# Gated linear attention and a mixer on one core: batch 2's scaled q and k turned by transposing transfers, with a new hand-written order

## The chip, the cores and the metric

One Trainium2 chip, one of its cores. A core has a matrix engine (PE, with its weight loads PEld), three engines for elementwise work (DVE, ACT, POOL), a queue engine (SP) that here only issues transfers, and 16 DMA engines that move data between HBM and the on-chip memory (SBUF). PE writes to eight banks of accumulator memory (PSUM), from which DVE and ACT copy results out. The metric is the device time of one execution in microseconds (us), lower is better; it is told as the median of several runs.

## What is computed

Four batches of 768 tokens. Per batch an attention with eight heads of 48 and a decaying state, then a mixer: two products over the tokens, a residual, two products over the channels, a residual.

```python
# attention: batch 4, heads 8, tokens 768, head size 48
f = 1.0 / (1.0 + np.exp(-f_logit))
for t in range(S):
    state = f[:, :, t, :, None] * state + einsum('bhd,bhe->bhde', k[:, :, t], v[:, :, t])
    y[:, :, t] = einsum('bhd,bhde->bhe', q[:, :, t], state)
# mixer on x = y as [4, 768, 384]; w_tok 768x256 and 256x768, w_ch 384x1536 and 1536x384
h = np.maximum(x.transpose(0, 2, 1) @ w_tok1, 0.0) @ w_tok2
u = x + h.transpose(0, 2, 1)
out = u + np.maximum(u @ w_ch1, 0.0) @ w_ch2
```

Inputs and output are float32; the products run in bf16 with float32 accumulation.

## The kernel before

Each batch's 768 tokens are six chunks of 128. For a chunk the kernel takes the logarithms of the gates (`gates`: Exp and Ln on ACT, and `Llo`, the low half of a split into two bf16 parts, by a subtraction on DVE or POOL) and sums them over the chunk's tokens by a product with a triangular matrix (the "sums", L516 to L531). From the sums ACT makes two factors, `G` and `Gi` (L541, L543). DVE multiplies q by the one and k by the other into the tile `qk` (L562). Scores within the chunk need q and k with the head dimension on the partitions, so `qk`, 128 tokens by 1024, must be turned into `qkT`. There are two ways in the code:

- on PE (L579): eight 128x128 products with the identity into one PSUM bank, which DVE then copies to `qkT` (L592);
- by a transposing transfer (L569), issued on SP, from `qk` straight to `qkT`. A placeholder on PE that issues nothing (`hold`) reserves the PSUM bank that the scores will use.

`TURNED` says from which batch on the second way is taken: 3, so batch 3 alone. Then come the scores (L476), their masking on DVE (`AmT`, L616), the products of k and v for the state (`parts`, L492), the state's update on DVE (L628 to L633) and its copies (`state_bd`), and the output `y` (L651, L658). The state needs the last row of the chunk's factor spread over the partitions in another way; from batch 1 on ACT writes it to `ends` (L550) and a small transfer on SP carries it over to `glast` (L556, called `across`). Batches 1 to 3 handle chunks in pairs.

The mixer of a batch (`mixer`) has the token products (L693, L709), the residual (L725), a copy to bf16 (`u_bf`), a turn of it to `uT` (on PE and DVE for batches 0 and 1, by two transfers, L739, for batches 2 and 3), the first channel product with its ReLU (`ch1`, L768, L439 and L441), and the second (`ch2`, L787) with residual (L793) and output (L797, 192 KB per tile of 128 tokens, on SP).

The inputs are loaded by POOL in a fixed sequence (L360, L367); batch 0's gates by SP and ACT. There are four sets of `qk`/`qkT`, taken by the chunk's number modulo 4: chunks 0 to 3 take sets 0 to 3, chunks 4 and 5 sets 0 and 1, and the next batch begins with set 0 again.

Work is not issued where it is written down. Every piece of work is an operation with its possible engines, what it needs and makes, and a cost (`kind`), and gets a running number. The table `ORDER`, written out by hand, lists all 1116 operations: code // 4 is the operation's number, code % 4 picks one of its engines. `best` goes through `ORDER`, gives each operation a start by the costs, gives out the PSUM banks, and fills gaps on PE before 25.5 us with dummy products (L834). The operations are then issued in the order of these starts. Each engine works strictly in its order and waits at an operation until what it needs is there. So on one engine the order is that of `ORDER`; the costs act only on the choice of banks and on the number of dummies. Cost entries that matter here: `("fix", own, end)` occupies its engine for `own` ns and is done after `end`; a fourth number made a transfer occupy a common wire.

Of the kernel before, what the change touches and what calls it, by code (L numbers as in the profile page):

```python
# [20 lines left out]
TURNED = 3  # L21
ORDER = (
# [60 lines left out]
)  # L83
KEPT = 3
SPLIT = 5
SLOTS = (5110, 5800, 7500, 8450, 9600, 10400, 11400, 13000, 14400, 14800, 16700,
         18000, 19100, 19500, 20000, 20700, 21400, 23400, 24300, 25900)
HELD = (2600, 3600, 4100, 4750, 5500, 6500)


class Op:
# [18 lines left out]
class Plan:  # L110
# [65 lines left out]
    def best(self, idle, cold, until):  # L176
# [10 lines left out]
        for code in ORDER:  # L187
# [47 lines left out]
            elif op.kind[0] == "fix" and len(op.kind) > 3:  # L235
                wire = max(wire, t + 1000) + op.kind[3]
                if op.kind[3] > 1000:
                    op.end = max(op.end, wire + 1200)
# [629 lines left out]
```

## Time and profile before

| | |
|---|---|
| time, median of 3 runs | 172.79 us (171.46 to 176.41) |
| span of the profiled execution | 170.2 us |
| granted PE clock in it | 1.000 |
| instructions | 4181 |
| HBM read, written | 25.17 MB, 4.72 MB |
| busy POOL | 99.3 us (58%) |
| issue of one transposing transfer, `qkT`, on SP | 1.31 us, median of 6 |
| issue to landing of an output tile, `across`, `uT` | 3.1, 4.0, 2.8 us, medians |

The profile shows one execution. The span runs from the first to the last instruction; the measured times also hold what lies around it. "Busy" is the time in which an engine had work, and PE's pieces overlap in its pipeline, so the latency of one product is longer than the distance between two. A row of a group reads: line, engine, operation, what is written and read, how often; then busy us and mean ns of one; then how long the engine had been idle before, and on what. For a transfer the landing is counted from its issue.

### The profile page before, as it was taken

The numbers are of one execution on the slowest core, as the hardware profiler recorded it, in microseconds if no ns is written. First come the engines' busy times: TensorE is split into PE (matmuls) and PEld (weight loads), VectorE is DVE, ScalarE is ACT, GpSimd is POOL, SyncE is SP. The second block draws the span as 40 slices with busy tenths as digits, with TensorE's granted clock in tenths as the row PEclk, the third lists the DMA queues.
The fourth block names the chain that finished last, engine by engine and source line by source line (L and its number), as shares of the span: only waits on it lengthen the run. The fifth ranks groups of instructions, "written<-read, shape, count | busy, mean of one in ns | idle before, by whom it ended". The sixth has DMA issues, their size and how long they took to land.

```text
span 170.2 us, 4181 instructions
## 1 busy us (share of the span) xinstructions
PE 162.9 (96%) x1606; PEld 102.8 (60%) x1606; DVE 128.0 (75%) x287; ACT 108.2 (64%) x256; POOL 99.3 (58%) x134
## 2 busy tenths in 40 slices
PE   6899999999999999999999999999999999999992
PEld 2356565665766576665776756665666666566661
DVE  5679995966898998899999868768884723675431
ACT  4759993598879889999999978385545320510100
POOL 7999569896499969999978869603111200000000
PEclk9999999999999999999999999999999999999999
DMA  6999999999999997999998999996920060220253
GB/s 103 141 174 149 156 192 181 212 149 201 192 167 136 161 165 75 116 155 133 182 157 49 134 251 107 144 165 115 228 100 4 0 139 0 92 96 0 78 202 139
DMA packets 102547, 22.71 MB, mean 133 GB/s; under 512 B 95264, under 2 KB 101664, under 8 KB 102528
## 3 DMA queue, kind: packets, MB, share of 16 engines
q0 software_dynamic: 79440, 13.77, 101.8%
q1 hardware_dynamic: 22560, 8.59, 22.5%
q8 instruction: 12, 0.20, 0.5%
q10 hardware_dynamic: 528, 0.10, 0.3%
q14 instruction: 7, 0.06, 0.1%
HBM read 25.17 MB, written 4.72 MB: 176 GB/s over the span
## 4 chain that ended last, share of the span: by engine, by line
PE 64%; DMA 12%; DVE 7%; ACT 6%; POOL 6%; issue 2%; SPq 1%; DVEq 0%; POOLq 0%
PE ps L768 22%; PE ps L787 22%; DMA v_sb<-in_v_dram 5%; PE ps L709 4%; POOL qk_sb L360 4%; PE ps L693 4%; DMA glast<-ends 4%; DMA out_dram<-x_nat 3%; DVE AmT L616 2%; PE ps L476 2%; PE ps L579 2%; PE ps L658 2%; POOL v_sb L360 1%; PE ps L530 1%; PE ps L651 1%
## 5 line engine op out<-in xcount | busy, mean ns | idle before, releaser
L787 PE MATMUL ps<-w_ch,zT 128*128 128x384 bf16 (+2 forms) x300 | 51.6, 320 | 0.0
L768 PE MATMUL ps<-uT,w_ch 128*128 128x384 bf16 x288 | 50.6, 326 | 0.0
L439 ACT ACTIVATE zT<-ps 128x384 bf16<-128x384 f32 x56 | 25.3, 494 | 25.3 <-PE ps L768 25.2
L768 PEld LDWEIGHTS <-w_ch 128*128 128x128 bf16 x288 | 27.7, 98 | 17.7
L787 PEld LDWEIGHTS <-zT 128*128 128x128 bf16 x300 | 27.9, 98 | 16.9
L616 DVE TENSOR_TENSOR AmT<-ps,tri_bf 128x512 bf16<-128x512 f32 x46 | 30.5, 686 | 2.5 <-PE ps L476 2.3
L441 DVE TENSOR_SCALAR zT<-ps 128x384 bf16<-128x384 f32 x40 | 21.1, 554 | 8.8 <-PE ps L768 8.8
L360 POOL DMA_DIRECT2D v_sb<-in_v_dram x24 | 22.2, 925 | 4.1 <-DMA w_ch<-in_moe_w_ch_dram 4.1
L360 POOL DMA_DIRECT2D qk_sb<-in_k_dram x24 | 22.4, 932 | 0.8 <-POOLq L852 0.8
L360 POOL DMA_DIRECT2D qk_sb<-in_q_dram x24 | 22.3, 930 | 0.0
L793 DVE TENSOR_TENSOR x_nat<-x_nat,ps 128x384 f32<-128x384 f32 (+2 forms) x25 | 13.3, 535 | 10.6 <-PE ps L787 10.2
L360 POOL DMA_DIRECT2D f_sb<-in_f_logit_dram x18 | 16.5, 943 | 0.2
L562 DVE TENSOR_TENSOR qk<-qk_sb,GG 128x768 bf16<-128x768 bf16 (+1 forms) x30 | 14.2, 475 | 2.1 <-ACT GG L543 1.0
L450 ACT ACTIVATE f_sb<-f_sb 128x384 f32<-128x384 f32 x24 | 12.5, 524 | 4.6 <-DMA f_sb<-in_f_logit_dram 4.4
L434 POOL CAST state_bd<-state 48x192 bf16<-48x192 f32 x13 | 4.5, 347 | 16.2 <-DVE state L633 14.6
L725 DVE TENSOR_TENSOR x_nat<-x_nat,ps 128x384 f32<-128x384 f32 x21 | 10.5, 550 | 3.4 <-PE ps L709 3.1
L834 PE MATMUL ps<-steady 128*128 128x512 bf16 x30 | 11.3, 483 | 1.7 <-DVE steady L375 1.7
L543 ACT ACTIVATE GG<-ps 128x384 bf16<-128x384 f32 x24 | 11.6, 489 | 2.0 <-PE ps L531 1.9
L541 ACT ACTIVATE GG<-ps 128x384 bf16<-128x384 f32 x24 | 11.7, 488 | 1.4 <-PE ps L531 1.2
L579 PE MATMUL ps<-ident,qk 128*128 128x128 bf16 x144 | 11.6, 224 | 0.0
L579 PEld LDWEIGHTS <-qk 128*128 128x128 bf16 x144 | 9.2, 100 | 2.7 <-DVE qk L562 0.7
L550 ACT ACTIVATE ends<-ps 32x384 f32<-32x384 f32 x15 | 7.0, 481 | 4.9 <-PE ps L531 4.7
(81 smaller groups left out, 234.1 us busy)
## 6 DMA issues: line engine op xcount, KB each, us to landing
out_dram<-x_nat SPq DMA_DIRECT2D x23, 192.0 KB, 3.1
f_sb<-in_f_logit_dram POOLq DMA_DIRECT2D x18, 192.0 KB, 5.4
qk_sb<-in_k_dram POOLq DMA_DIRECT2D x24, 96.0 KB, 5.1
qk_sb<-in_q_dram POOLq DMA_DIRECT2D x24, 96.0 KB, 4.9
v_sb<-in_v_dram POOLq DMA_DIRECT2D x24, 96.0 KB, 5.5
w_ch<-in_moe_w_ch_dram POOLq DMA_DIRECT2D x2, 576.0 KB, 7.5
w_ch<-in_moe_w_ch_dram POOLq DMA_DIRECT2D x1, 1152.0 KB, 10.6
f_sb<-in_f_logit_dram SPq DMA_DIRECT2D x5, 192.0 KB, 4.7
```

What stands on the lines that cost most here:

```text
L360: lambda eng=eng, into=into, of=of: eng.dma_start(out=into, in_=of),
L439: nc.scalar.activation(out_, in_, AF.Relu, bias=0.0, scale=1.0)
L441: nc.vector.tensor_scalar(out_, in_, 0.0, None, ALU.max)
L450: add(ACT, r, lambda: nc.scalar.activation(fb, fb, AF.Exp, bias=0.0, scale=-1.0), make=[key], kind=el, need=([("fb", c)] if c < 1 else []) ...
L541: add(ACT, r, lambda: nc.scalar.activation(G[i], sview(), AF.Exp, bias=0.0, scale=-1.0), make=[("G", i)], bank=p_s, kind=el)
L543: add(ACT, r, lambda: nc.scalar.activation(Gi[i], sview(), AF.Exp, bias=0.0, scale=1.0), make=[("Gi", i)], bank=p_s, kind=el)
L562: add(DVE, r, lambda n=n: nc.vector.tensor_tensor(qk[i4][:, n, :, 0:D], qk_sb[nb][:, n, :, c, :], GG[i][:, n], ALU.mult), need=[(x, nb, c) ...
L579: nc.tensor.transpose(to[:, o + hp, :], blk(src)[:, hp, :], ident)
L616: add(DVE, r, lambda half=half, made=made: nc.vector.tensor_tensor(half, made(), tb4, ALU.mult), need=["tri_bf"], make=[("AmT", i, p)], ba ...
L768: nc.tensor.matmul(banks[pm.at][:, 0:384], lhsT=w[:, kt, c0:c0 + 128], rhs=uT[:, th, :, kt, :], start=(kt == 0), stop=(kt == 2))
L787: nc.tensor.matmul(banks[pm.at][:, 0:n1 - n0], lhsT=zT[:, kt, tt * 128:(tt + 1) * 128], rhs=w_ch2[:, kt, n0:n1], start=(kt == 0), stop=(kt ...
L793: add(DVE, rank("ch2", tt), lambda un=un, pm=pm, n=n1 - n0: nc.vector.tensor_tensor(un, un, banks[pm.at][:, 0:n], ALU.add), make=[("x_nat" ...
```

## The change

- `TURNED` is 2 instead of 3: batch 2's `qk` is turned by transposing transfers too. Its six chunks lose eight products on PE and one DVE copy each, and get one transfer on SP and one placeholder on PE.
- The placeholder no longer needs the transfer, so it may reserve its bank before the transfer has landed.
- The sets of `qk`/`qkT` are numbered through the batches, `(b * NCH + c) % NQ` with `NQ = 4`, so that a set comes around every four chunks also where one batch follows another.
- In the planner transfers of a `fix` kind no longer occupy a common wire; they have fixed landing times, with new numbers for `across`, the transposes and the outputs, and a transpose of the mixer's or the attention's kind waits in the plan for the last but one before it.
- `ORDER` is new as a whole. The numbers of the operations mean what they meant, except that in each chunk of batch 2 the two operations of the turn are now a transfer and a placeholder, and that in batch 3 these two have changed places.

```diff
-TURNED = 3
+TURNED = 2
+NQ = 4
 ORDER = (
...
 )
...
+        turned: list = []
...
+            if op.kind[0] == "fix" and len(op.kind) > 3 and len(turned) > 1:
+                t = max(t, turned[-2])
...
-            elif op.kind[0] == "fix" and len(op.kind) > 3:
-                wire = max(wire, t + 1000) + op.kind[3]
-                if op.kind[3] > 1000:
-                    op.end = max(op.end, wire + 1200)
+            elif len(op.kind) > 3 and op.kind[0] == "fix":
+                turned.append(op.end)
...
-        need = [("qkT", c % 4, p) for c in cs for p in range(2)]
+        need = [("qkT", (b * NCH + c) % NQ, p) for c in cs for p in range(2)]
...
-        i, i4, nb, g4 = c % 2, c % 4, b % NB, (b * NCH + c) % 4
+        i, i4, nb, g4 = c % 2, (b * NCH + c) % NQ, b % NB, (b * NCH + c) % 4
...
-                kind=("fix", 600, (5200, 5200, 3400)[b - 1], 300))
+                kind=("fix", 500, (6000, 5200, 4500)[b - 1]))
...
         if b >= TURNED:
+            add(SP, r, lambda: nc.sync.dma_start_transpose(out=qkT[i4], in_=qk[i4].rearrange("t n h d -> t (n h d)")),
+                need=[("qh", i4), ("kh", i4)], make=[("qkT", i4, 0), ("qkT", i4, 1)], kind=("fix", 1350, 6500, 1))
             hold = Bank()
-            add(SP, r, lambda: nc.sync.dma_start_transpose(out=qkT[i4], in_=qk[i4].rearrange("t n h d -> t (n h d)")),
-                need=[("qh", i4), ("kh", i4)], make=[("qkT", i4, 0), ("qkT", i4, 1)], kind=("fix", 1900, 6000, 1700))
-            add(PE, r, lambda: None, need=[("qkT", i4, 0)], make=[("hold", b, c)], bank=hold, kind=("mm", 1))
+            add(PE, r, lambda: None, make=[("hold", b, c)], bank=hold, kind=("mm", 1))
             return [hold, Bank()]
...
-                make=[("uT", 3 * th + j, d) for j in range(3) for d in range(3)], kind=("fix", 1900, 6000 if b > 2 else 8000, 1900))
+                make=[("uT", 3 * th + j, d) for j in range(3) for d in range(3)], kind=("fix", 1400, 4000 if b > 2 else 7200, 1))
...
-                    need=[("x_nat", xn, tt, n0) if end else ("x_nat", xn, tt)], kind=("fix", 350, 2000, 580))
+                    need=[("x_nat", xn, tt, n0) if end else ("x_nat", xn, tt)], kind=("fix", 420, 4500 if b < 3 else 2000))
```

What the new `ORDER` holds that the prediction speaks of, read from its codes:

- Eight ReLUs of batch 1 are given to DVE instead of ACT, two of batch 0 too; in batches 2 and 3 five go from DVE to ACT. In batch 0, two copies to `qkT`, one of `y`, one of `u_bf` and one of `uT` go from DVE to ACT, and one of the state's copies from ACT to DVE. In batches 2 and 3 four of the copies to `x_bf` go from DVE to ACT.
- On PE the order of the stages is as before, with other interleaving. Between the sums of batch 2's chunk 1 and the scores of chunks 0 and 1 stand one token product (two products), 18 turns of `u_bf`, the sums of chunks 2 and 3 and 14 `ch1` groups of three products.
- On SP, the transfers around batch 2 run: transpose of chunk 0, its `across`, output of batch 0's tile 5, transpose of chunk 1, output of tile 4, `across` of chunk 2, transposes of chunks 2 and 3, `across` of chunks 1 and 3, transposes of chunks 5 and 4, `across` of chunk 4, output of batch 0's tile 3, transposes of batch 3's chunks 0 and 1.
- On POOL the loads keep their sequence. The two `Llo` of batch 2 that POOL makes are those of chunks 2 and 3, before those of chunks 1 and 0.
- The last group on PE is the third part of batch 3's tile 0, 384 columns, with its residual and output behind it; before, it was tile 5's last 96 columns.

More of the change, by code (lines that the diff above doesn't have):

```diff
@@ L300 @@
     G, Gi = [t[:, 0] for t in GG], [t[:, 1] for t in GG]
-    qk = [st([128, 2, H, 64], BF16, f"qk{i}") for i in range(4)]
+    qk = [st([128, 2, H, 64], BF16, f"qk{i}") for i in range(NQ)]
     qh, kh = [t[:, 0] for t in qk], [t[:, 1] for t in qk]
-    qkT = [st([128, 8, 128], BF16, f"qkT{i}") for i in range(4)]
+    qkT = [st([128, 8, 128], BF16, f"qkT{i}") for i in range(NQ)]
     AmT = [st([128, 8, 128], BF16, f"AmT{i}") for i in range(2)]
@@ L411 @@
         once(DVE, lambda i=i: nc.vector.memset(state_bd[i], 0.0), [("sbd", i)], 220)
-    for i in range(4):
-        once(DVE, lambda i=i: nc.vector.memset(ends[i][96:128, :, D:64], 1.0), [("ends", i)], 200)
+    for i in range(NQ):
+        if i < 4:
+            once(DVE, lambda i=i: nc.vector.memset(ends[i][96:128, :, D:64], 1.0), [("ends", i)], 200)
         for n, tl in (("qh", qh[i]), ("kh", kh[i])):
@@ L480, in attention @@
             own = 212 if k else 330
-            chain = add(PE, due(b, cs[0]), lambda c=c, k=k: scores(c % 4, heads[k]), need=need, bank=heads[k][1],
+            chain = add(PE, due(b, cs[0]), lambda c=c, k=k: scores((b * NCH + c) % NQ, heads[k]), need=need, bank=heads[k][1],
                         kind=("mm", own if live and b else own + 107, own), tail_of=chain)
@@ L491, in parts @@
                     hp, par = h // 2, h % 2
-                    nc.tensor.matmul(dg(k)[par * 64:par * 64 + 64, hp, :], lhsT=kh[c % 4][:, h, :],
+                    nc.tensor.matmul(dg(k)[par * 64:par * 64 + 64, hp, :], lhsT=kh[(b * NCH + c) % NQ][:, h, :],
                                      rhs=v_sb[nb][:, h, c, :], start=b > 0 or (c == 0 and hp == 0), stop=True,
@@ L496, in attention @@
         if live and b == 0:
-            add(PE, due(b, cs[0]), parts, need=[("kh", cs[0] % 4), ("v", nb, cs[0])], make=["sums"], bank=p_d,
+            add(PE, due(b, cs[0]), parts, need=[("kh", cs[0] % NQ), ("v", nb, cs[0])], make=["sums"], bank=p_d,
                 kind=("mm", 345, 238))
         elif live:
-            chain = add(PE, due(b, cs[0]), parts, need=[("kh", c % 4) for c in live] + [("v", nb, c) for c in live],
+            chain = add(PE, due(b, cs[0]), parts, need=[("kh", (b * NCH + c) % NQ) for c in live] + [("v", nb, c) for c in live],
                         bank=p_d, kind=("mm", 230 + 115 * len(live), 123 + 115 * len(live)), tail_of=chain)
@@ L597, in rest @@
     def rest(b, c, r, p_a, p_d, dg):
-        i, i4, nb, g4 = c % 2, c % 4, b % NB, (b * NCH + c) % 4
+        i, i4, nb, g4 = c % 2, (b * NCH + c) % NQ, b % NB, (b * NCH + c) % 4
         last = c == NCH - 1
```

120 rows, old and new, of the table ORDER are left out of this document.

## The prediction

> **What bounds the kernel now.** I read the page first, then the busy time by stretch.
>
> ```profile
> span 170.2 us, 4181 instructions
> PE 162.9 (96%) x1606; PEld 102.8 (60%) x1606; DVE 128.0 (75%) x287; ACT 108.2 (64%) x256; POOL 99.3 (58%) x134
> ```
>
> ```profile
> 0.00:20.00 20.00, 17.52 (x183) 9.10 (x183) 15.41 (x52) 13.67 (x34) 17.32 (x28) 1.00 1.90 142
> 20.00:25.00 5.00, 4.82 (x87) 3.40 (x84) 4.74 (x13) 4.80 (x12) 3.02 (x5) 1.00 1.61 187
> 25.00:32.00 7.00, 6.51 (x67) 4.14 (x66) 5.09 (x12) 4.20 (x11) 6.87 (x9) 1.00 1.14 209
> ...
> 45.00:60.00 15.00, 14.61 (x181) 9.73 (x180) 13.68 (x30) 12.43 (x30) 14.84 (x18) 1.00 2.13 154
> 60.00:75.00 15.00, 14.87 (x170) 10.03 (x169) 14.01 (x32) 14.19 (x36) 13.54 (x17) 1.00 1.52 127
> 75.00:90.00 15.00, 15.00 (x192) 10.35 (x192) 14.60 (x32) 14.71 (x37) 13.37 (x17) 1.00 1.86 150
> ...
> 120.00:135.00 15.00, 14.76 (x150) 9.47 (x149) 10.91 (x24) 6.85 (x15) 2.65 (x8) 1.00 0.37 88
> ...
> 150.00:166.90 16.90, 16.83 (x116) 10.50 (x113) 8.49 (x18) 1.36 (x3) 0.00 (x0) 1.00 0.29 108
> 166.90:170.20 3.30, 0.00 (x0) 0.00 (x0) 0.22 (x1) 0.00 (x0) 0.00 (x0) 1.00 0.32 110
> ```
>
> PE is busy for 96% of the span. Columns of the second fence: stretch, length, then busy PE, weight loads, DVE, ACT, POOL, the granted clock and the DMA share. There are three parts. Up to about 32 us PE is not the limit: it is filled up with L834 dummies (11.3 us, row below) while loads, DVE and ACT deliver batch 0. From 32 to 166.9 PE never rests: its idle time in the rows from 25 us on is 0.49 + 0.39 + 0.13 + 0.24 + 0.07 = 1.3 us, at full clock. The last 3.3 us are the tail: last residual, last output. So a microsecond of PE work removed after 32 us is worth a microsecond, as long as what replaces it arrives in time. In 60 to 90 us there is little room beside PE: DVE is busy 28.6 of 30 us, ACT 28.9.
>
> **What is removed.** Batch 2's scaled q and k are turned on PE (L579, eight 128x128 per chunk) and copied out by DVE (L592).
>
> ```profile
> L579 PE MATMUL ps<-ident,qk 128*128 128x128 bf16 x144 | 11.6, 224 | 0.0
> L592 DVE COPY qkT<-ps 128x1024 bf16<-128x1024 bf16 x12 | 7.7, 685 | 0.4 <-PE ps L579 0.4
> L834 PE MATMUL ps<-steady 128*128 128x512 bf16 x30 | 11.3, 483 | 1.7 <-DVE steady L375 1.7
> L441 DVE TENSOR_SCALAR zT<-ps 128x384 bf16<-128x384 f32 x40 | 21.1, 554 | 8.8 <-PE ps L768 8.8
> ```
>
> ```profile
> 32.22 7.80 PE ps L768 x48
> 69.66 0.45 PE ps L579 x8
> 88.48 0.89 PE ps L579 x16
> ```
>
> The 224 ns is the latency of one; in the chain eight take 0.45 us and sixteen 0.89. Six chunks of eight: 6 x 0.45 = **-2.7 us of PE**, all of it between 69 and 90 us, where PE is the bound. DVE loses six copies, 6 x 0.685 = 4.1 us. The new order spends part of that at once: counting the engine chosen by each code, eight ReLUs of batch 1 go from ACT to DVE, and over the whole program ReLUs on ACT fall from 56 to 51 while ACT takes over copies of qkT and x_bf. DVE ends nine instructions lighter, ACT equal, POOL three heavier (small casts). I cost this rearrangement at nothing: PE covers it where the rows above leave it idle at most 0.13 us, and each stretch keeps DVE below PE.
>
> **What is added: six transposing transfers on SP.**
>
> ```profile
> L569 SPq DMA_TRANSPOSE qkT<-qk x6: 1245/1308/4509, 97.2 to 117.1; - x6
> DMA to landing us min/median/max: 3.1/3.7/7.5
> ```
>
> The issue, 1.3 us each, is on SP, which has time. What counts is the way from the gate sums to the scores. Read from the new order, the tightest is chunks 0 and 1. Between the end of chunk 1's sums and the scores PE does 48 matmuls of 384 columns (42 of L768, four sums, two of token mixing) and 18 turns: 48 x 7.80/48 + 18 x 0.89/16 = 8.8 us. In that time ACT makes Gi, the first chunk's ends row and G (three of about 0.45 us: 25.3/56 from the first row here), DVE multiplies (14.2/30 = 0.47), and SP, free by then of chunk 0's transpose and one output, issues.
>
> ```profile
> L439 ACT ACTIVATE zT<-ps 128x384 bf16<-128x384 f32 x56 | 25.3, 494 | 25.3 <-PE ps L768 25.2
> L562 DVE TENSOR_TENSOR qk<-qk_sb,GG 128x768 bf16<-128x768 bf16 (+1 forms) x30 | 14.2, 475 | 2.1 <-ACT GG L543 1.0 <-ACT GG L541 0.9
> ```
>
> With 0.4 us of semaphore steps that is 2.3 us, so 6.5 us are left from issue to landing. For chunks 4 and 5 the same count gives 11.2 us, of which DVE's four masks ahead of the multiply and the two issues leave about 6.9; chunks 2 and 3 have over 10. Batch 3's first pair keeps about 8. Now the landing time at 70 to 95 us, which the trace has only for other transfers. The DMA view by window (q0 carries POOL's loads, q1 what SP issues: packets, MB, share of the 16 engines; then an issue with its size and landing) has in 70 to 80 us
>
> ```profile
> q0 software_dynamic: 8803, 1.25, 180.0%
> ```
>
> ```profile
> out_dram<-x_nat SPq DMA_DIRECT2D x1, 192.0 KB, 4.3
> ```
>
> in 107 to 115 us
>
> ```profile
> q1 hardware_dynamic: 3357, 1.00, 91.3%
> q0 software_dynamic: 2997, 0.28, 76.7%
> ```
>
> ```profile
> qkT<-qk SPq DMA_TRANSPOSE x2, 7.0
> ```
>
> and in 115 to 120 us
>
> ```profile
> q0 software_dynamic: 37, 0.00, 1.3%
> ```
>
> ```profile
> qkT<-qk SPq DMA_TRANSPOSE x2, 3.2
> ```
>
> Without loads a transpose lands in 3.2 us; beside loads, and one output and two other transposes on its own queue, in 7.0. An output under the full load took 4.3 us against 1.9 in the quiet tail (row below): 2.26 times, and 3.2 x 2.26 = 7.2. Both ways give 7.0 to 7.2. Bounds: 3.2 and, if the wait goes with q0's share, 12.3 (in a rival below). I take 7.0, by the row with the same operation, so PE waits 7.0 - 6.5 = **+0.5 us** once; nothing is queued behind the scores on PE that could go ahead. At 3.2 us it is 0.
>
> Two rules of the Trainium skill bear on it. "DMA: Bandwidth & Descriptors", section "Queues, rings and completion order", says that each DMA engine takes the queue rows in turn, a packet at a time. By that a transpose keeps a half share however long the load queue is, 6.4 us as an estimate, and the wait would be 0. "VectorE: DVE Perf Modes", section "Rules for kernel authors", would have a 128x128 turned on TensorE where PSUM will do as destination, and speaks against this change; the trace agrees that the transfer is the slower way (3.2 us at best against 0.45 + 0.685), but it is PE's time that is scarce here. What that rule would cost is the late-transfer rival.
>
> **What is moved.** Numbering the sets through the batches makes each use of qk and qkT four chunks apart, also over a batch's end, where it was two; that takes a wait away or does nothing. The planner's constants act through the order alone. The hold on the PSUM bank no longer waits for the transfer and issues nothing. POOL's loads keep their sequence; its two Llo of batch 2 move from chunks 0 and 1 to 2 and 3, behind eight loads more, and the b2c2 sums come about 4 us of PE work sooner: no gain, no more than 0.5 us of loss, inside the range. On SP, batch 0's outputs are spread anew; the transposes of batch 2 stand behind outputs of batch 0 whose residuals are long done.
>
> The tail changes. Today it ends with tile 5 in 288 and 96 columns, so that the last residual and transfer are small. In the new order the last PE group is tile 0 of 384 columns, and some seven outputs are issued within the last 4 us.
>
> ```profile
> 166.87 0.26 DVE x_nat L793
> ```
>
> ```profile
> L793 DVE TENSOR_TENSOR x_nat<-x_nat,ps 128x384 f32<-128x384 f32 (+2 forms) x25 | 13.3, 535 | 10.6 <-PE ps L787 10.2
> ```
>
> ```profile
> out_dram<-x_nat SPq DMA_DIRECT2D x8, 192.0 KB, 1.9
> ```
>
> ```profile
> out_dram<-x_nat SPq DMA_DIRECT2D x1, 48.0 KB, 1.6
> ```
>
> ```profile
> L797 SPq DMA_DIRECT2D out_dram<-x_nat x2: 537/582/628, 120.5 to 121.1; - x2
> DMA to landing us min/median/max: 5.2/5.3/5.3
> ```
>
> The residual costs 0.535 - 0.26 = 0.3 more, the landing 1.9 - 1.6 = 0.3 more if the queue is clear; six outputs issued in a row around 120 us landed in 5.3, 3.7 more. Here the earlier ones start up to 3 us ahead of the last and are mostly through. I take 0.2 for them, nearest to the tail's own rows: **+0.8**, bounds 0.6 and 4.0.
>
> **Sum.** 170.2 - 2.7 + 0.5 + 0.8 = 168.8 us of span. The median of the three runs, 172.79, is 2.6 above the span (the lowest, 171.46, is 1.3); with 2.6 the forecast is 171.4.
>
> **Rivals.**
>
> More than the turns is gained. The idle 1.3 us from 25 us on go, and the start shortens: in 20 to 25 us DVE and ACT are busy 4.74 and 4.80 of 5 us, so they, not PE's dummies, set when the mixer begins, and the order moves five instructions of batch 0 from DVE to ACT and three back. Up to 1 us there, as an estimate two instructions' worth. With the short tail: 170.2 - 2.7 - 1.3 - 1.0 + 0.6 = 165.8, and 168.4 as a time. Against it: ACT is as full as DVE there.
>
> Late transfers, slower than before. If landing goes with the load queue's share, it grows by (7.0 - 3.2)/(76.7 - 1.3) per point and reaches 12.3 us at 180%. PE then waits at the first pair (landing - 6.5) and again at the third (landing - 6.9), since the third is issued after the first wait. It decides from 8 us on, where the two waits, 2.6 in all, reach the 1.9 us gained; at 10 us they are 3.5 + 3.1: 170.2 - 2.7 + 0.8 + 6.6 = 174.9, and 177.5 as a time. For it: 7.5 at a share of 77%, and one issue that held SP for 4.5 us. Against it: the output under full load only doubled.
>
> Nothing moves. DVE bounds 60 to 90 us once PE gets shorter: its 28.6 us lose 4.1 of copies and gain eight ReLUs of 21.1/40 = 0.53, which makes 28.7, or 29.3 with steps between that it cannot fill (0.6, under half of the 1.4 us it idles there now). Then 0.7 of the 2.7 us remain and the tail takes them: 172.8 - 0.7 + 0.8 = 172.9.
>
> **Chances.** Forecast 0.38 (its own range 169 to 173), more gained 0.25, late transfers 0.27, nothing moves 0.10. A measurement of this kernel can tell about 2% from no change: below 169.3 or above 176.2. Below lies most of the second case (0.22) and the lower edge of the first (0.12): 0.34. Above lies most of the third (0.20) and 0.01 for the rest: 0.21. Between: 0.45. The range goes from 167.8, under the second case, to 176.5, short of the third's far end; some 0.2 is left out.
>
> **What would show it.** L579 with 96 instead of 144 instructions and about 7.8 us busy, L592 with six; L569 with twelve, those between 70 and 95 us landing in about 7 us; weight loads of L476 waiting for a DMA at the first pair of batch 2, for half a microsecond in all; the L768 rows at 32 us starting where they do now; after the last matmul 4.1 us instead of 3.3. Landings over 8 us with PE idle twice in 75 to 95 us would bring in the late-transfer case; PE idle behind DVE or ACT there, the last one; a first L768 before 31.5 us, the second.

## The result: slower, and where the time went

The changed kernel takes 178.22 us as the median of four runs (177.65 to 179.82), the kernel before 172.14 beside it: a ratio of 1.037, with a 95% interval of 1.030 to 1.045. Its profiled execution took 178.43 us, 1.7 more than its span. Medians here are of all runs of a kernel; the ratios leave disturbed runs out, which is why a ratio can be lower than its medians say.

(One correction to what stands ahead of the prediction: in batch 3 the transfer and the placeholder have the same numbers as before; only the placeholder's wait for the transfer is gone.)

The page of the changed kernel, its busy time by stretch (columns as in the prediction), and what PE waited for (total, times, longest):

```profile
span 176.7 us, 4088 instructions
...
PE 160.7 (91%) x1553; PEld 99.5 (56%) x1553; DVE 124.7 (71%) x278; ACT 109.0 (62%) x256; POOL 101.5 (57%) x137
...
L771 PE MATMUL ps<-uT,w_ch 128*128 128x384 bf16 x288 | 51.7, 330 | 5.0 <-ACT GG L546 4.8
...
L582 PE MATMUL ps<-ident,qk 128*128 128x128 bf16 x96 | 7.9, 220 | 2.6 <-DVE qk L565 2.3
```

```profile
75.00:90.00 15.00, 11.28 (x115) 7.00 (x114) 10.20 (x23) 8.51 (x20) 10.69 (x13) 1.00 1.71 153
90.00:105.00 15.00, 13.17 (x146) 8.20 (x146) 11.79 (x25) 12.33 (x30) 10.55 (x15) 0.89 1.90 147
...
85.00:90.00 5.00, 2.03 (x29) 1.42 (x28) 1.30 (x3) 0.32 (x1) 1.86 (x3) 1.00 1.47 138
90.00:95.00 5.00, 3.17 (x11) 1.52 (x11) 2.55 (x5) 4.07 (x10) 2.34 (x3) 0.66 2.59 125
```

```profile
PE ps L771 <- ACT GG L546: 4.8, 1, 4.8
...
PE ps L479 <- DMA qkT<-qk: 0.7, 1, 0.7
```

The turns are gone as intended (L582, L579 before, has 96 instructions). But PE, which never rested from 75 to 90 us, now works 11.28 of those 15 us. Most of the gap is one wait of 4.8 us, which runs on past 90 us, and it is not a wait for a transpose: PE's matmul waits for a PSUM bank that ACT's L546 (Gi) has to read first. The wait for a transpose is there too, 0.7 us, where it was forecast.

Why was ACT late? Its timeline (start, us, engine, line, what, and in brackets the idle time before and what ended it), and the load in the chain of waits:

```profile
84.83 0.50 ACT L546 ACTIVATE GG<-ps 128x384 bf16<-128x384 f32 x1
90.88 0.52 ACT L453 ACTIVATE f_sb<-f_sb 128x384 f32<-128x384 f32 x1 [5.56 <-DMA f_sb<-in_f_logit_dram]
91.31 0.47 ACT L546 ACTIVATE GG<-ps 128x384 bf16<-128x384 f32 x1
```

```profile
79.12 11.74 DMA f_sb<-in_f_logit_dram
```

ACT takes its instructions in order. The new order has the Exp (L453) of batch 3's chunk 0 ahead of the last Gi of batch 2. ACT stands 5.56 us before that Exp, because the chunk's gate load, issued at 79.12, landed 11.74 us later. Loads issued at that time landed in 5.1 us in the kernel before, and in 11.6 now (issues in 76.5 to 78 us of the kernel before, then in 79 to 80.5 of the changed one: count, KB, median us to landing):

```profile
f_sb<-in_f_logit_dram POOLq DMA_DIRECT2D x2, 192.0 KB, 5.1
```

```profile
f_sb<-in_f_logit_dram POOLq DMA_DIRECT2D x2, 192.0 KB, 11.6
```

What else was under way then shows in SP's timeline and in the transposes' own landing times (those issued in 71 to 82 us):

```profile
71.70 1.33 SPq L571 DMA_TRANSPOSE qkT<-qk  x1
...
74.40 2.87 SPq L571 DMA_TRANSPOSE qkT<-qk  x1
...
78.69 5.35 SPq L571 DMA_TRANSPOSE qkT<-qk  x2
...
92.44 4.07 SPq L571 DMA_TRANSPOSE qkT<-qk  x2
```

```profile
DMA to landing us min/median/max: 3.5/9.5/11.9
```

Four transposes lie over POOL's loads, and both are slow: that the one makes the other slow is what the experiments have to show. To split the span, take L771's first start and the end of the last matmul, here for the kernel before and then for the changed one:

```profile
L768 PE MATMUL ps<-uT,w_ch x288: 322/326/336, 32.1 to 160.0; 128*128 128x384 bf16 x144
```

```profile
161.92 4.90 PE L787 MATMUL ps<-w_ch,zT 128*128 128x384 bf16 x40
```

```profile
L771 PE MATMUL ps<-uT,w_ch x288: 322/326/524, 33.3 to 161.9; 128*128 128x384 bf16 x144
```

```profile
168.43 4.72 PE L790 MATMUL ps<-w_ch,zT 128*128 128x384 bf16 x31
```

Before: 32.1 to 166.8, then 3.4 of tail. After: 33.3 to 173.15, then 3.6. So the start lost 1.3 us, the tail 0.2, and the middle went from 134.8 to 139.8 where 134.8 - 2.7 + 0.5 = 132.6 was expected. The same middle, with each run's span, is the measure of all experiments. Span and middle are of one profiled execution each; the ratio is of several runs, against runs of the kernel before made beside them:

| run | span | first L771 to PE's end | ratio to before (95%) |
|---|---|---|---|
| before | 170.2 | 134.8 | |
| after | 176.7 | 139.8 | 1.037 (1.030 to 1.045) |
| no_b2_transfer | 171.7 | 132.1 | 0.995 (0.990 to 0.999) |
| plain_copy | 169.8 | 133.6 | 0.997 (0.993 to 1.002) |
| exp_behind_gi | 175.8 | 138.8 | 1.031 (1.023 to 1.039) |
| f_ahead | 178.8 | 141.8 | 1.046 (1.037 to 1.054) |
| extra_transfers | 182.6 | 147.3 | 1.072 (1.067 to 1.077) |
| only_c2_c3 | 170.1 | 133.7 | 1.007 (1.000 to 1.014) |
| c2_c3_on_pe | 171.2 | 134.0 | 1.010 (1.000 to 1.020) |
| old_start_c2_c3_on_pe | 171.4 | 135.2 | 1.001 (0.996 to 1.006) |
| c0_to_c3 | 177.1 | 139.9 | 1.046 (1.040 to 1.053) |
| no_kqv_b3 | 176.6 | 139.4 | 1.041 (1.038 to 1.045) |
| new_order_on_pe | 171.3 | 134.8 | 1.013 (1.007 to 1.019) |
| no_kqv_b2c4_c5 | 167.6 | 131.9 | 0.988 (0.983 to 0.993) |

### The profile page after: what moved, and what is told of

It reads as the page before. It is cut to its first block, busy times and chain, and to the rows that moved or that the text cites. A ratio compares the mean times of both kernels' runs of the same rounds, so it can differ in the third digit from the quotient of the medians.

```text
span 176.7 us, 4088 instructions
## 1 busy us (share of the span) xinstructions
PE 160.7 (91%) x1553; PEld 99.5 (56%) x1553; DVE 124.7 (71%) x278; ACT 109.0 (62%) x256; POOL 101.5 (57%) x137
## 4 chain that ended last, share of the span: by engine, by line
PE 34%; DMA 26%; POOL 26%; issue 6%; ACT 3%; DVE 3%; POOLq 0%; DVEq 0%
PE ps L771 15%; PE ps L790 14%; POOL qk_sb L362 11%; DMA f_sb<-in_f_logit_dram 11%; DMA w_ch<-in_moe_w_ch_dram 10%; POOL v_sb L362 7%; DMA qk_sb<-in_k_dram 5%; POOL f_sb L362 4%; POOL Llo L460 2%; PE ps L696 1%; PE ps L712 1%; DVE AmT L619 1%; PE ps L479 1%; DVE qk L565 1%; ACT qkT L433 1%
## 5 line engine op out<-in xcount | busy, mean ns | idle before, releaser
L771 PE MATMUL ps<-uT,w_ch 128*128 128x384 bf16 x288 | 51.7, 330 | 5.0 <-ACT GG L546 4.8
L790 PE MATMUL ps<-w_ch,zT 128*128 128x384 bf16 (+2 forms) x300 | 53.2, 322 | 0.2 <-DVE tsum L634 0.2
L771 PEld LDWEIGHTS <-w_ch 128*128 128x128 bf16 x288 | 27.9, 99 | 23.9 <-issue 6.9
L790 PEld LDWEIGHTS <-zT 128*128 128x128 bf16 x300 | 28.5, 98 | 18.2 <-issue 1.1
L444 DVE TENSOR_SCALAR zT<-ps 128x384 bf16<-128x384 f32 x45 | 23.7, 554 | 12.0 <-PE ps L771 9.9
L442 ACT ACTIVATE zT<-ps 128x384 bf16<-128x384 f32 x51 | 22.9, 493 | 14.2 <-PE ps L771 13.8
L453 ACT ACTIVATE f_sb<-f_sb 128x384 f32<-128x384 f32 x24 | 12.4, 522 | 11.7 <-DMA f_sb<-in_f_logit_dram 11.6
L437 POOL CAST state_bd<-state 48x192 bf16<-48x192 f32 x15 | 5.2, 344 | 17.6 <-DVE state L636 10.9
L433 ACT ACTIVATE x_bf<-ps 128x384 bf16<-128x384 f32 x19 | 9.0, 487 | 8.3 <-PE ps L661 8.3
L546 ACT ACTIVATE GG<-ps 128x384 bf16<-128x384 f32 x24 | 11.6, 490 | 1.9 <-PE ps L534 1.3
L696 PE MATMUL ps<-x_bf,w_tok 128*128 128x384 bf16 x48 | 10.9, 325 | 0.3 <-ACT x_bf L433 0.2
L582 PE MATMUL ps<-ident,qk 128*128 128x128 bf16 x96 | 7.9, 220 | 2.6 <-DVE qk L565 2.3
L837 PE MATMUL ps<-steady 128*128 128x512 bf16 x25 | 8.6, 461 | 1.7 <-DVE steady L377 1.7
```

The lines of the kernel that those rows point to most:

```text
L442: nc.scalar.activation(out_, in_, AF.Relu, bias=0.0, scale=1.0)
L444: nc.vector.tensor_scalar(out_, in_, 0.0, None, ALU.max)
L453: add(ACT, r, lambda: nc.scalar.activation(fb, fb, AF.Exp, bias=0.0, scale=-1.0), make=[key], kind=el, need=([("fb", c)] if c < 1 else []) ...
L546: add(ACT, r, lambda: nc.scalar.activation(Gi[i], sview(), AF.Exp, bias=0.0, scale=1.0), make=[("Gi", i)], bank=p_s, kind=el)
L696: add(PE, rank("tok1", rt), lambda rt=rt, kt=kt, pm=pm: nc.tensor.matmul(banks[pm.at][:, 0:DM], lhsT=w_tok1[:, kt, rt * 128:(rt + 1) * 128 ...
L771: nc.tensor.matmul(banks[pm.at][:, 0:384], lhsT=w[:, kt, c0:c0 + 128], rhs=uT[:, th, :, kt, :], start=(kt == 0), stop=(kt == 2))
```

## The experiments

Theory: the transposes of batch 2 take DMA time from POOL's loads; a load that then lands late holds an engine that works in order. Rivals: the new order is slower by itself; ACT's order alone is at fault; PE waits for the transposes.

**No transfers in batch 2** (no_b2_transfer), the new order otherwise untouched:

```diff
-add(SP, r, lambda: nc.sync.dma_start_transpose(...
+add(SP, r, (lambda: None) if b == 2 else lambda: nc.sync.dma_start_transpose(...
```

> The changed kernel without the six transfers of batch 2: its scores read what an earlier chunk left in qkT, so this part is not computed; order, waits and all else stay. Theory (the transfers take DMA time from POOL's loads, and the Exp of batch 3's first chunk then waits for its load in ACT's in-order queue): the loads issued at 78 to 82 us land in about 5 us instead of 12, ACT's wait of 5.56 us before the Exp goes, and with it PE's 4.8 and 0.7 us and the lower clock behind them; span 169 to 171 us instead of 176.7. Rival (the new order is slower by itself): the load's wait at the Exp and PE's idle time stay to at least half, span 174 or more.

In its profiled execution the granted clock was 0.91 in the first 20 us and 0.71 in the five after, and L771 began only at 35.6; so only what lies behind is read. The middle took 132.1 us, 2.7 under the kernel before. ACT's wait at the same Exp:

```profile
86.77 0.52 ACT L453 ACTIVATE f_sb<-f_sb 128x384 f32<-128x384 f32 x1 [0.28 <-DMA f_sb<-in_f_logit_dram]
```

0.28 us instead of 5.56; the two gate loads landed in about 5.5 us. So the six transfers cost 139.8 - 132.1 = 7.7 us (by the ratios (1.037 - 0.995) x 172 = 7.2), against the 2.7 of PE's turns that they replace. The DMA view of 82 to 90 us (queue, packets, MB, share of 16 engines), first without them, then with:

```profile
q0 software_dynamic: 7561, 1.10, 188.9%
q1 hardware_dynamic: 268, 0.00, 2.9%
```

```profile
q0 software_dynamic: 3260, 0.67, 102.1%
q1 hardware_dynamic: 1971, 0.48, 62.7%
```

In the same eight microseconds POOL's queue moved 4301 packets less and SP's queue 1703 more, mostly of transposes: 2.5 packets of loads for one. The figure depends on the window, since the two runs issue their gate loads 2.03 us apart: over eight microseconds from that issue on (79 to 87 with them, 81 to 89 without) it is 3981 less and 1786 more, 2.2 for one. The packets differ in size. In the trace most of the loads' packets have 96 bytes and most of the transposes' 256, and in the fences above the loads lost 0.43 MB while SP's queue gained 0.48. "DMA: Bandwidth & Descriptors" of the Trainium skill, section "Queues, rings and completion order", has each engine take the queues in turn, a packet at a time. The loads did give up places, as that rule has it; whether the packets counted here are that rule's packets no run shows, so the exchange of one for one is neither borne out nor refuted.

**Plain copies** (plain_copy), the same 256 KB from qk to qkT:

```diff
+add(SP, r, (lambda: nc.sync.dma_start(out=qkT[i4]..., in_=qk[i4]...)) if b == 2 else ...
```

> The six transfers of batch 2 as plain copies of the same 256 KB from qk to qkT, without the turning (the scores of batch 2 are not computed rightly). If what burdens the loads is the transposing form: loads at 78 to 82 us land in 5 to 7 us, span 169 to 172. If any transfer of 256 KB at this place does it: loads land in about 12 us, span 175 to 178.

```profile
L571 SPq DMA_DIRECT2D qkT<-qk x6: 491/492/593, 70.6 to 87.3; - x6
L571 SPq DMA_TRANSPOSE qkT<-qk x6: 1232/1282/2190, 94.5 to 120.4; - x6
```

The middle loses 1.5 us (half a microsecond or less by the ratios) where the transposes lose 7.7; the gate loads land in 7.2 us and ACT waits 1.8. It is chiefly the transposing form that burdens the loads. The page's totals of SP's queue (packets, MB, the packets' time as a share of 16 engines' span) are, without batch 2's transfers, with copies and with transposes:

```profile
q1 hardware_dynamic: 22560, 8.59, 21.8%
q1 hardware_dynamic: 23424, 10.16, 25.2%
q1 hardware_dynamic: 28896, 10.16, 30.5%
```

So a copy has 144 packets and a transpose 1056. With the spans of 171.7, 169.8 and 176.7 us the shares make 599, 685 and 862 us of DMA engine time: 86 us for six copies, 263 for six transposes, three times as much for the same bytes. How much of a packet's time is waiting beside others, these totals don't tell. "Advanced Engine Details and Errata" of the Trainium skill, section "X-Bar Transpose (TRN2)", states that transposing DMAs are as fast as regular ones. The rows above don't agree: the issue alone takes 1.28 us instead of 0.49, the first four copies landed in 4.8 us (median) where the transposes took 9.5, and the same bytes cost the kernel five times as much.

**The Exp later in ACT's order** (exp_behind_gi): Exp and Ln of batch 3's chunk 0 behind the x_bf of batch 2's chunk 0.

```diff
-    ... 2428, 2928, 3496, 2960, ... 2756, 3500, 2764, ... 1988, 2724, 3508, ...
+    ... 2428, 2928, 2960, ... 2756, 2764, ... 1988, 2724, 3496, 3500, 3508, ...
```

> The changed kernel with the Exp and Ln of batch 3's chunk 0 moved back in ACT's order, behind the last gates and the copies of batch 2's chunks 0 and 1. Theory: the load still lands at about 91 us, but G and Gi of batch 2 no longer stand behind it; PE's 4.8 us at L771 go, about 2 us come back where PE needs the sums of batch 3's chunk 0; span 172.5 to 175. Rival (the loads of batch 2's own last chunk, which land as late, hold the same work): PE's idle time only moves, span 176 to 177.5.

From PE's timeline, two rows with a wait:

```profile
91.66 0.33 PE L533 MATMUL ps<-f_sb,tri_bf 128*128 128x384 bf16 x1 [0.63 <-ACT f_sb L455]
92.56 0.48 PE L534 MATMUL ps<-Llo,tri_bf 128*128 128x384 bf16 x1 [0.58 <-POOL Llo L460]
```

The single wait of 4.8 us is gone. These two stand in its place, with 0.83 at 89.81 and 1.22 at 103.87; 1 us came back of the 2 to 4 that the theory expected, nearer to its rival, by which PE's idle time only moves. So ACT's order is where the late load is felt, not what makes it late: DVE waits 1.82 us for q of chunk 5 as well.

**The gate loads earlier** (f_ahead): two codes moved in POOL's order.

```diff
-    ... 476, 480, 484, ... 488, ... 492, 1964, 1968, 2708, ...
+    ... 476, 480, 1964, 1968, 484, ... 488, ... 492, 2708, ...
```

> The changed kernel with the gate loads of batch 3's chunks 0 and 1 issued ahead of k, q and v of batch 2's chunk 5. Theory: the two loads land by about 84 us and ACT's 5.56 us go, but the transfers take as much from the queue as before, so k and q of chunk 5 land at about 90 us and DVE's multiply for it waits instead; span 173 to 176. Rival (only the place of the two loads in the queue was wrong): all of PE's 4.8 us come back, span 170 to 172.

The gate loads land by 86.3 us and ACT no longer waits for them, but now DVE does, and PE for a residual that stands behind the waiting multiply on DVE:

```profile
90.91 2.26 DVE L565 TENSOR_TENSOR qk<-qk_sb,GG 128x768 bf16<-128x768 bf16 x2 [3.98 <-DMA qk_sb<-in_q_dram]
```

```profile
94.16 1.05 PE L479 MATMUL ps<-qkT 48*128 48x128 bf16 x15 [4.22 <-DVE x_nat L796]
```

The wait moved to q of chunk 5, as the theory said, but at a higher price than it said: 141.8 us, 2 more than the changed kernel. That only the place of these two loads was wrong is ruled out.

**Six more transposes in the kernel before** (extra_transfers), with nobody waiting for their result; batch 2 is still turned on PE, in the old order:

```diff
 nc.sync.dma_start(out=glast[g4], in_=ends[g4][127:128]...)
+for j in range(c, c + (2 if c == 4 else 1)) if b == 2 else ():
+    ...
+    nc.sync.dma_start_transpose(out=old[:, at:at + 1024]..., in_=w_ch2...[:, 0:1024])
```

> The kernel before, with batch 2 still turned on PE, and six transposing transfers more in batch 2, issued on SP behind the glast transfers; they read w_ch2 and write where batch 1's q, k and v were, and nobody waits for them. Theory (the transfers slow POOL's loads, whoever uses them): landings of the loads issued behind the third or fourth of them rise from 4 or 5 us to 8 us or more, PE waits somewhere between 75 and 105 us, span 172 to 177 instead of 170.2. Rival (only the wait for their result, or the new order, costs time): loads and span unchanged, 170 to 170.8.

```profile
70.33 1.34 SPq L560 DMA_TRANSPOSE v_sb<-w_ch  x1
...
72.61 2.31 SPq L560 DMA_TRANSPOSE v_sb<-w_ch  x1
```

```profile
80.20 0.52 ACT L450 ACTIVATE f_sb<-f_sb 128x384 f32<-128x384 f32 x1 [4.36 <-DMA f_sb<-in_f_logit_dram]
```

```profile
82.73 4.08 PE L773 MATMUL ps<-uT,w_ch 128*128 128x384 bf16 x15 [4.33 <-ACT GG L543]
```

```profile
DVE state L638 <- DMA glast<-ends: 5.0, 1, 5.0
```

Two transposes, issued at 70 and 73 us, and the kernel before shows the fault of the changed one: the gate loads issued at 70 and 71 us land 9.8 us later instead of 5.3, ACT stands 4.36 us before an Exp, PE 4.33 behind ACT's next gate. This is neither the new order nor a wait for a transpose's result. The whole loss of 12.5 us (147.3 - 134.8) isn't all of this kind: the glast transfers stand behind the transposes on SP, and DVE waits 5.0 us for one (last fence). It is more than the 2 to 7 us expected.

**Which of the six** (only_c2_c3, c0_to_c3, c2_c3_on_pe). The first two leave out the transfers of the other chunks, whose scores are then computed from what was left in qkT; the third turns chunks 2 and 3 on PE again, with their codes moved in the order to fit.

```diff
+add(SP, r, (lambda: None) if b == 2 and c not in (2, 3) else lambda: ...   # only_c2_c3
+add(SP, r, (lambda: None) if b == 2 and c > 3 else lambda: ...             # c0_to_c3
-if b >= TURNED:
+if b > TURNED or b == TURNED and c not in (2, 3):                          # c2_c3_on_pe
```

> The changed kernel with the transfers of batch 2's chunks 2 and 3 alone; those of chunks 0, 1, 4 and 5 are left out, and their scores read what was left in qkT. Theory (two transfers issued at 79 and 81 us fall into the burst of POOL's loads and displace them): most of the loss stays, loads of batch 3's chunk 0 land in 8 to 11 us, span 172.5 to 175.5 against about 169.5 with none and 176.7 with all six. Rival (it takes all six, or the first two, whose results PE waits for): span 169 to 171.

> The changed kernel with batch 2's chunks 2 and 3 turned on PE and copied by DVE again, the other four by transfer. Theory: the loads at 78 to 82 us land in 5 to 7 us, ACT's wait before the Exp falls under 1.5 us, 0.9 us of PE work come back; span 170 to 172.5. Rival (any of the transfers does it): 174 to 177.

> The changed kernel with the transfers of batch 2's chunks 0 to 3 and none for chunks 4 and 5 (their scores read what was left in qkT). Chunks 2 and 3 alone cost 1.5 us between the first L771 and PE's end, all six 7.7. Theory (each transfer puts back the queue of loads, the delays add up, and only what goes beyond the slack of a load's user costs time; in the changed kernel the transfers of chunks 4 and 5 were issued behind the long wait and can't have caused it): the wait before the Exp and PE's wait at L771 stay at 3 to 5 us, 4 to 6 us are lost, span 173 to 176. Rival (the loss goes evenly with the number, or comes of the last two): 1.5 to 3 us lost, span 170.5 to 172.5.

Against 132.1 us with none, chunks 2 and 3 alone lose 1.6 us in the profile, not the "most of the loss" expected of them. That reading is weak: the profiled run, 171.77 us, was the fastest of ten, whose median is 175.12 and whose slowest took 180.12. By the ratios it is (1.007 - 0.995) x 172 = 2.1. Chunks 0, 1, 4 and 5 lose 134.0 - 132.1 - 2 x 0.45 = 1.0 (1.7 by the ratios); ACT's wait is 1.02 us there, as expected. Chunks 0 to 3 lose 7.8, more than the 4 to 6 expected and as much as all six; the waits are those of the changed kernel:

```profile
PE ps L771 <- ACT GG L546: 5.0, 1, 5.0
```

```profile
90.98 0.52 ACT L453 ACTIVATE f_sb<-f_sb 128x384 f32<-128x384 f32 x1 [5.72 <-DMA f_sb<-in_f_logit_dram]
```

So by these profiles the delays do not cost in proportion, 1.6 and 1.0 apart and 7.7 together; with the spread of the first run this is likely rather than shown. A reading that fits, and that no run tests by itself: each transfer puts the loads back, what two do is still mostly covered by the lead that the loads have, and with four in a row the lead is used up and every further microsecond is paid. The last two cannot have had a part: in the changed kernel they were issued at 92.44, behind the long wait.

**The old start** (old_start_c2_c3_on_pe): the run above with the order of the kernel before up to batch 0's first L771.

> The kernel of the run above, with the old order up to the first matmul of batch 0's channel mixing. If the later start is the order of batch 0: the first L771 at about 32.1 us instead of 33.3 and the span 0.5 to 1.2 us shorter than in the run above, 169 to 171.5. Otherwise the same as the run above.

Its first L771 is at 32.5 us against 33.5, but its middle is longer by as much; the span is 171.4 against 171.2. Runs with the new order ahead of batch 2 begin L771 between 32.1 and 33.6 us (35.6 in the one with the low clock at the start), so the start can't be laid at the order's door by one profile of each. This stays open.

**Less traffic for POOL** (no_kqv_b3: batch 3's k, q and v are not loaded and batch 0's are used; no_kqv_b2c4_c5: those of batch 2's chunks 4 and 5 are set to 1.0 by POOL in their place):

```diff
-    lambda eng=eng, into=into, of=of: eng.dma_start(out=into, in_=of),
+    (lambda: None) if b == 3 and n != "f" else lambda ...                                      # no_kqv_b3
+    (lambda into=into: nc.gpsimd.memset(into, 1.0)) if b == 2 and c > 3 and n != "f" else ...  # no_kqv_b2c4_c5
```

> The changed kernel with all its transfers, but without batch 3's loads of k, q and v (batch 3 is computed from what batch 0 left there). Theory (transfers and loads take from each other): with 18 loads fewer the two gate loads of batch 3's chunks 0 and 1 land in 5 to 7 us, the transfers of chunks 2 and 3 in 5 to 8 us instead of 11 and 12, ACT's wait before the Exp is under 2 us; span 169 to 172. Rival (the transfers are slow by themselves, or the order is): landings of the transfers and PE's idle time stay, span 174 or more.

> The changed kernel with all its transfers, and k, q and v of batch 2's chunks 4 and 5 set to 1.0 by POOL in the place of their six loads (batch 2's last two chunks are computed from that). These loads stand ahead of batch 3's gate loads in the queue, where the 18 left out in the earlier run stood behind. Theory (loads land in the order of the queue, and the transfers put back the whole queue): with six loads fewer ahead, the gate loads of batch 3's chunks 0 and 1 land in 4 to 7 us, ACT's wait before the Exp is under 1.5 us and PE's wait at L771 under 1; span 169 to 172.5. Rival (while the transfers run a load takes 11 us whatever stands ahead of it): the waits stay, span 174 or more.

The first expectation failed: the two gate loads still took about 11 us, ACT waited 5.88 us, and the theory as it was put there fell. All 18 loads left out stand behind the gate loads in POOL's queue, and taking them away frees nothing ahead. With the six loads ahead of them gone, and the gate loads issued 4.7 us sooner for it, the same six transposes do no harm (landing of the gate loads issued in 74 to 76 us, then the busy times in 75 to 90 us, both of no_kqv_b2c4_c5):

```profile
f_sb<-in_f_logit_dram POOLq DMA_DIRECT2D x2, 192.0 KB, 5.1
```

```profile
75.00:90.00 15.00, 14.95 (x165) 9.40 (x162) 14.39 (x31) 13.47 (x33) 10.92 (x15) 1.00 1.59 166
```

PE has no gap, and the middle is 131.9 us. In this kernel the harm takes both, the transposes and the loads ahead in the queue. How much of the gain is the shorter queue and how much the earlier issue, this run doesn't separate.

**The new order with batch 2 on PE** (new_order_on_pe): TURNED = 3 again, each turn put ahead of the matmuls before its scores, each copy behind it on DVE.

> The changed kernel with all of batch 2 turned on PE and copied by DVE again: the new order, numbering and constants, without the six transfers. Theory (the transfers alone made it slower): first L771 to PE's end at 132.1 + 2.7 = 134.8 us, as before the change, to 136 where DVE's six copies don't fit; span 170.5 to 173. Rival (the order costs a part): span 174 or more.

134.8 us in the middle, to a tenth what the kernel before takes and what 132.1 + 2.7 makes. Order, numbering and the planner's constants cost the middle nothing in this profile. They cost some at the ends: L771 begins at 32.4 instead of 32.1, and the tail is 4.0 instead of 3.4; the ratio is 1.013. Of the runs that leave nothing out, none was faster than the kernel before.

## Why the prediction was wrong

It forecast 171.4 us and a range up to 176.5; the kernel takes 178.2. By its own steps:

- *The turns, -2.7.* Right: 132.1 us without turns and transfers, 134.8 with turns.
- *The wait of the first pair, +0.5.* 0.7 us, at the place named, but partly by luck. Chunk 1's transpose landed in 8.0 us, not 7.0 (chunk 0's in 3.5), and the room was larger too: issued at 74.40, it could have been used from 81.8 on, 7.4 us and not 6.5. The two errors nearly cancel. No run shows the 0.4 us of semaphore steps in that sum; from the end of chunk 1's sums (71.85) to the issue it took 2.6 us, where 2.3 was counted.
- *The tail, +0.8.* The last matmul group is as forecast; the tail grew by 0.2 in the changed kernel and by 0.6 with the new order on PE, so the lower bound was nearer.
- *The start unchanged.* It is 1.3 us later in this profile. No term stood for it.
- *2.6 us from span to time.* Every execution here whose span is on record has 1.7 or 1.8 between them. The 2.6 was a median set against the span of another execution; it made the forecast 0.9 too high.
- *"What counts is the way from the gate sums to the scores."* This is the step that failed. It priced a transpose by when its result arrives, and never by what it takes from the loads that are under way. The landing rows quoted beside it gave a hint, read the other way round: where two transposes took 7.0 us beside loads instead of 3.2, the loads could be expected to lose as well. The price is 7.7 us, and no term of the sum held it.
- *"POOL's loads keep their sequence."* The sequence was kept, the landings were not: 11.7 us for the decisive one, and the sum had nothing for it.
- *The rearrangement of ACT and DVE costed at nothing, since PE covers it.* Nothing names there which ACT instruction waits for a load and what is queued behind it. That is how a late load reached PE. The order alone is not at fault: without transfers that wait is 0.28 us.

The rival of late transfers, with a chance of 0.27, came near in time (177.5) and had the sign; its mechanism was not this one. The transfers of chunks 2 and 3 did land in over 8 us, its deciding point, but neither they nor those of the third pair held PE; its idle time came from a load, through ACT. The change does to batch 2 what it says; the account is 1.3 at the start, -2.7 for the turns, +7.7 for what the transfers take, 0.2 for the tail: 6.5 us of span, from 170.2 to 176.7.

Of the 7.7, PE's idle time explains most. PE is busy for 133.5 of the 139.8 us of the changed kernel's middle, and for 131.8 of the 132.1 without the transfers: 6.0 us more are idle. The other 1.7 us are the same work done more slowly, at a granted clock of 0.96 from 75 to 120 us where it is 1.00 without the transfers; 0.04 x 45 = 1.8 agrees.

Two of the rules that the prediction weighed bear on this case. The rule of turns per packet gave a half share to the transpose and no wait; its estimate of 6.4 us to landing stands against 8.0 for chunk 1, and its other side, that the loads then give up some of theirs, is the kind of price that was missing. And the one in "VectorE: DVE Perf Modes" of the Trainium skill, section "Rules for kernel authors", that a 128x128 is turned on TensorE where PSUM will do, holds for this kernel even though PE is its bound: 134.8 us with PE's turns against 139.8.

Not settled: why a transpose takes three times the DMA engine time of a copy; the start; and how much of the loss a spacing of the transposes between the loads would save, which was not tried.

## What to carry to other kernels

A transfer has two prices: when its own result arrives, and what everything else under way loses meanwhile; where the DMA engines are as busy as here (a share of 1.86 in 75 to 90 us before the change), work out the second from the lead of the loads that land there. Then look, for each load, at which engine waits for it in order and what is queued behind that instruction, since that is what stops. A delay within the lead can be free and the next equal one not: in this kernel the six transposes cost 7.7 us with the full load queue ahead and nothing that shows with six loads fewer. A transfer that relieves the busiest engine is better placed where the load queue is nearly empty, as it was under the last of batch 3's transposes, which landed in 3.2 us before the change.

## What the hardware showed beside this

A transpose costs far more than its bytes: 1056 packets for 256 KB against 144 for the plain copy, 44 us of DMA engine time against 14, 1.28 us of issue on SP against 0.49, and 3.35 us of issue for the slowest, with the next glast transfers behind it.

The granted clock fell behind long gaps of PE. After the 4.8 us it was 0.66 in 90 to 95 us and 1.00 again from 95 on; where PE idled 4.16 of the five microseconds from 90 to 95 (f_ahead), it was still 0.59 in the five after:

```profile
90.00:95.00 5.00, 0.84 (x15) 0.73 (x14) 4.09 (x7) 0.66 (x2) 2.58 (x3) 0.73 2.63 142
95.00:100.00 5.00, 5.00 (x40) 2.72 (x37) 4.27 (x10) 2.07 (x6) 2.37 (x4) 0.59 1.24 124
```

So such a gap is paid for twice, once idle and once at the lower clock behind it. A short one need not be: in the run with plain copies, where PE waited 1.1 us at the same place, the clock stayed at 1.00.
